# A rarely taken branch moved from the middle of a mixture-of-experts kernel to its end, and four gathers moved within GpSimd's order

## The chip, the cores and the metric

The kernel runs on one core of a Trainium2 chip. The core has TensorE (PE: matmuls, and PEld: weight loads), VectorE (DVE), ScalarE (ACT), GpSimd (POOL) and SyncE (SP, which issues the transfers), each with its own instruction stream. The metric is the device time of one execution in microseconds (us); lower is better.

## The reference

Pooled attention over 4 batches of 576 tokens gives `x` of 2304 rows and 512 columns. A mixture of 8 experts follows, of which each token takes its best two, then a dense mixture of 4 experts. All is float32.

```python
# attention: k and v averaged over 8 neighbours, softmax(q k / 8) v -> x [2304, 512]
logits = x @ w_gate
noisy_logits = logits + np.log1p(np.exp(x @ w_noise)) * noise
top2 = np.argpartition(-noisy_logits, 2, axis=1)[:, :2]   # softmax of the two -> top2_w
for e in range(8):                                        # first mixture
    for k in range(2):
        mask = top2[:, k] == e
        h = np.maximum(x[mask] @ w1[e], 0.0)              # 512 -> 1024
        out[mask] += top2_w[mask, k, None] * (h @ w2[e])  # 1024 -> 512
for e in range(4):                                        # second mixture, x is out
    out2 += p[:, e:e + 1] * (np.maximum(x @ w1[e], 0.0) @ w2[e])
```

## The kernel before, in words

**Stages.** Attention writes `x` to a buffer `x_d` in memory. A routing step on VectorE finds each token's two experts and gives it a slot in a table of 8 times 640 slots (`CAP`). Then come chunks, one after the other: tokens of one expert are gathered from `x_d` by GpSimd (`fetch1`, which calls `gather`), turned by TensorE (`turn_full`, `turn_plain`), multiplied by the expert's first matrix (layer 1), passed through the maximum with 0, and multiplied by the second (layer 2). Results of the first mixture go to a buffer `y_d`; `fetch2` gathers two rows for each token from it and `mix2` adds them. The second mixture works on three groups of 768 tokens and stores `out` (line 1144).

**Operands in two parts.** Each float32 operand is split into a rounded part and a remainder, and three products of them are summed. For weights, ScalarE writes the rounded part and GpSimd (or VectorE) subtracts it for the remainder. Some chunks use seven products of half matrices in place of eight (`run_seven`, `layer1_seven`): for these GpSimd first combines quarters of the weights in a tile `comb` (lines 561 to 564), ScalarE rounds (lines 566 and 574), and GpSimd subtracts (lines 570 to 580). First-layer weights lie in a ring of three tiles, `u0`, `u1` and `u2` (`u_161`, `u_162` and `u_163` in the rows of the program's order); second-layer weights lie in `v` and `v_last`.

**What sets the order.** The program is written out by hand: each engine executes its instructions in the order in which the Python code emits them. A chunk has two halves, each a row of places `u`; `add(h, u, f, ...)` enters a call at half `h`, place `u`. `ahead_plain` and the tables `AHEAD_1`, `AHEAD_2` say at which place which part of the next weights is split. `step` takes a routing generator to its next `yield`, so a `yield` more shifts what comes behind it by one place. SyncE waits, in order, for the data of each transfer that it issues.

**The branch.** If an expert gets more tokens than slots, the table doesn't hold them. The routing writes a flag `over` (line 473), and `general` (line 1111) reads it on each engine and, if it is set, runs `all_experts`, a loop over all tokens and all experts. `between` holds it until the matmuls of the second product of expert 7's first chunk are emitted (lines 697 and 1117). On the path on which the flag is 0, TensorE, VectorE and SyncE add to their semaphores what the skipped block would have added; SyncE does this with eight increments, one for each semaphore of its transfers. In the profiled execution the flag is 0.

**The gathers of expert 3.** Line 1088 enters four of its five gathers at place (0, 4) of the second chunk of expert 1, so they stand ahead of the weight splits of the next chunk, expert 2. Their turns are at places 8 to 14 of expert 2's first half.

Of the kernel before, what the change touches and what calls it, by code (L numbers as in the profile page):

```python
# [8 lines left out]
FT = mybir.dt.float32  # L9
# [6 lines left out]
OP = mybir.AluOpType  # L16
# [7 lines left out]
N, DM = B * S, H * D  # L24
F = 1024
E1, E2 = 8, 4
# [5 lines left out]
CAP = SLOT_TILES * 128  # L32
# [27 lines left out]
def tile_attention_moe_moe(  # L60
# [12 lines left out]
    nc = tc.nc  # L73
# [6 lines left out]

    dram = ctx.enter_context(tc.tile_pool(name="dram", bufs=1, space=DRAM))
    x_d = dram.tile([N, DM], FT, name="x_d")
    wd_d = dram.tile([N, E1], FT, name="wd_d")
    y_d = dram.tile([E1 * CAP, DM], FT, name="y_d")
    psr = ctx.enter_context(tc.tile_pool(name="psr", bufs=2, space=PSUM, side="right"))

    consts = pool(ctx, "consts", 1)
# [244 lines left out]
    over = consts.tile([128, 1], I32, name="over")  # L332
# [8 lines left out]
    def routing(g, hold):  # L341
# [120 lines left out]
        if g == EARLY - 1 or last:  # L462
            slots[last] = consts.tile([128, HC], I32, name=f"slots{int(last)}")
            nc.vector.tensor_scalar(slots[last], slotf, float((N if last else GROUPS[EARLY] * 128) - 1), None, op0=OP.min)
            for e in range(1 if last else SPLIT):
                for c in range(3 if last else 2):
                    fetch1(e, 2 + c if last else c, not last)
            yield
        nc.vector.scalar_tensor_tensor(rows[:, a:b], ei[:, a:b], float(CAP), pf, op0=OP.mult, op1=OP.add)
        yield  # L470
        if last:
# [209 lines left out]
    def bank():  # L681
        return pm.tile([128, 512], FT, name="wn", bufs=4)

    between = []

    def layer1(q, f, xa, xb, n, bank=bank, hs=None):

        w = pair_weights(q, f // 2)
        p = bank()[:, :n]
        i = 0  # L690
        for a, b in TERMS:
            for kd in range(KD):
                qu = (0 if f % 2 else 1) if kd < 2 else (3 if f % 2 else 2)
                nc.tensor.matmul(p, w[:, a, qu, (kd % 2) * 128:(kd % 2 + 1) * 128],  # L694
                                 xc[(xa, xb)[kd // 2]][:, b, kd % 2, :n], start=i == 0, stop=i == 11)
                i += 1
        while between:
            between.pop()()
        relu_split(f, 0, n, p, hs)()

    h_first, y_first = [], []
# [252 lines left out]
    def run_seven(n, sink, fills):  # L954
        subs = 2 * n // 128
        for h in range(2):
            q = at_half[0]
            fl = {k[1]: list(f) for k, f in fills.items() if k[0] == h}
            for u, plan in (AHEAD_2 if n == CA else AHEAD_1).items():
                for i, k in plan:  # L960
                    fl.setdefault(u, []).append(lambda i=i, k=k: w_step(4 * q + i, k, None, False))
            w_step(4 * q + 2, 9)
            for pr in range(2):
                layer1_seven(q, pr, n, fl, 7 * pr)
                w_at["used1"] += 1
            for t in range(subs):
                for f in fl.get(14 + t, ()):
                    f()
                step(3, 1)
                sink(h, t, layer2(q, t))  # L970
            w_at["used2"] += 2
            at_half[0] += 1


    def new_acc():
        return moe.tile([128, DM], FT, name="acc", bufs=6)
# [27 lines left out]
    def all_experts():  # L1004

        wd, oh = (sx[i][:, 0, 0:NT * E1].rearrange("p (t e) -> p t e", e=E1) for i in range(2))
        for k in range(2):
            o = oh if k else wd
            nc.vector.tensor_tensor(o, exp_i.unsqueeze(1).to_broadcast([128, NT, E1]),
                                    ei[:, :, k].unsqueeze(2).to_broadcast([128, NT, E1]), op=OP.is_equal)  # L1010
            nc.vector.tensor_tensor(o, o, wt2[:, :, k].unsqueeze(2).to_broadcast([128, NT, E1]), op=OP.mult)
        nc.vector.tensor_add(wd, wd, oh)
        nc.sync.dma_start(wd_d.rearrange("(t p) e -> p t e", p=128), wd)
        x, xT, w0, w1, h0, h1 = (xf[0].rearrange("p k c -> p (k c)")[:, i * 512:(i + 1) * 512] for i in range(6))
        y = new_acc()
        wt = consts.tile([128, E1], FT, name="wd_t")
        with tc.For_i(0, N, 128) as r:
            nc.sync.dma_start(x, x_d[bass.ds(r, 128), :])
            nc.sync.dma_start(wt, wd_d[bass.ds(r, 128), :])
            p = psr.tile([128, 512], FT, name="tr")  # L1020
            for kd in range(KD):
                nc.tensor.transpose(p[:, kd * 128:(kd + 1) * 128], x[:, kd * 128:(kd + 1) * 128], ident)
            nc.vector.tensor_copy(xT, p)
            nc.vector.memset(y, 0.0)
            for e in range(E1):
                for f in range(FB):
                    w = (w0, w1)[f % 2]
                    if f % 2:
                        nc.sync.dma_start(w[:, 0:256], wa[e, 0][:, f - 1, 0:256])
                        nc.sync.dma_start(w[:, 256:512], wa[e, 0][:, f, 256:512])  # L1030
                    else:
                        nc.sync.dma_start(w[:, 0:256], wa[e, 0][:, f, 256:512])
                        nc.sync.dma_start(w[:, 256:512], wa[e, 0][:, f + 1, 0:256])
                    p = psr.tile([128, 512], FT, name="tr")
                    for kd in range(KD):
                        nc.tensor.matmul(p[:, :128], w[:, kd * 128:(kd + 1) * 128],
                                         xT[:, kd * 128:(kd + 1) * 128], start=kd == 0, stop=kd == KD - 1)
                    nc.vector.tensor_scalar((h0, h1)[f // 4][:, (f % 4) * 128:(f % 4 + 1) * 128], p[:, :128],
                                            0.0, None, op0=OP.max)
                p = pm.tile([128, 512], FT, name="p2", bufs=2)  # L1040
                for f in range(FB):
                    w = (w0, w1)[f % 2]
                    nc.sync.dma_start(w, wa[e, 1][:, f])
                    nc.tensor.matmul(p, (h0, h1)[f // 4][:, (f % 4) * 128:(f % 4 + 1) * 128], w,
                                     start=f == 0, stop=f == FB - 1)
                nc.vector.scalar_tensor_tensor(y, p, wt[:, e:e + 1], y, op0=OP.mult, op1=OP.add)
            nc.sync.dma_start(y_d[bass.ds(r, 128), :], y)
        nc.vector.memset(wt2[:, :, 0], 1.0)
        nc.vector.memset(wt2[:, :, 1], 0.0)
        for k in range(2):  # L1050
            nc.vector.tensor_scalar(rows[:, :, k], tok_i, float(N // 2), None, op0=OP.add)

    fills = {}

    def add(h, u, f, *a):
        fills.setdefault((h, u), []).append(lambda: f(*a))
# [28 lines left out]
    add(0, 1, turn_full, (2, 3), 3)  # L1085
    add(0, 2, turn_full, (2, 4), 4)
    for c in range(4):
        add(0, 4, fetch1, 3, c)
    for k, at_k in enumerate(((0, 3), (0, 4), (0, 4), (0, 5))):
        add(*at_k, sums, CS, (k,))  # L1090
    for m, at_m in zip(ORDER, ((0, 6), (1, 4), (1, 0), (1, 5), (1, 1), (1, 2), (1, 3))):
# [2 lines left out]
    for e in range(2, E1 - 1):  # L1094
# [13 lines left out]
                add(0, 0, fetch1, e + 1, c)  # L1108
                add(1, 14 + c, turn_plain, (e + 1, c), (S1, S2), c)
        run_seven(CS, sink1(e, 0), fills)  # L1110
    def general():
        with tc.If(nc.values_load(over[0:1, 0:1], min_val=0, max_val=1) != 0):  # L1112
            all_experts()

    e = E1 - 1
    fills.clear()
    add(0, 1, between.append, general)
    for c in range(2):
        add(0, 0, fetch1, e, 3 + c)
        add(0, 4 + c, turn_plain, (e, 3 + c), (S3, S4), c)  # L1120
# [12 lines left out]
    def sink2(e, accs, c0, first, last):  # L1133
        def sink(h, t, p):
            tok = c0 + t
            w = pe[:, tok, e:e + 1]
            if first and h == 0:
                accs[tok] = new_acc()
                nc.vector.tensor_scalar(accs[tok], p, w, None, op0=OP.mult)
            else:  # L1140
                a = accs[tok]
                nc.vector.scalar_tensor_tensor(a, p, w, a, op0=OP.mult, op1=OP.add)  # L1142
                if last and h:
                    nc.sync.dma_start(out[tok * 128:(tok + 1) * 128, :], a)
        return sink
# [19 lines left out]
    for sc in range(3):  # L1165
        es = range(1 if sc == 0 else 0, E2)
        for e in es:
            fills.clear()
            k = e - es[0]
            if sc < 2 and k < 2:  # L1170
                a, b, c = (6 * (sc + 1) + 3 * k + i for i in range(3))
                for t, f, m, u in ((a, (0, 10), (0, 16), (0, 17)), (b, (0, 10), (0, 17), (0, 18)),
                                   (c, (0, 19), (1, 14), (1, 15))):
                    add(*f, fetch2, t)
                    add(*m, mix2, t)
                    add(*u, turn2, t)
            if sc < 2 and e == E2 - 1:
                add(0, 18, sums, CA)
                window(CA)
            run_seven(CA, sink2(e, accs, 6 * sc, e == 0, e == E2 - 1), fills)  # L1180


def arrays_of(i):
# [44 lines left out]
```

## Time and profile before

| | |
|---|---|
| three runs | 1309.9, 1314.5, 1314.6 us, median 1314.5 |
| the profiled execution | 1311.17 us, its span 1309.4 us |
| TensorE matmul, weight load busy | 98%, 88% of the span |
| VectorE, ScalarE, GpSimd busy | 54%, 44%, 65% |
| transfers | 156.18 MB, 119 GB/s in the mean |
| granted TensorE clock | 0.998 of the full one |

The span reaches from the first to the last instruction of the program; the execution's own time has 1.8 us more around it. A busy share says little about the end of the time, as the stages have other limits each; below, stretches are looked at one by one. A "q" behind an engine's name (PEldq, SPq) is its sequencer, which issues instructions and is not counted as busy.

### The profile page before, as it was taken

Reading aid. Unit: us, or ns where it says so; the run is one execution under the profiler, and the core shown is the slowest. Engines: PE = TensorE matmul, PEld = TensorE weight load, DVE = VectorE, ACT = ScalarE, POOL = GpSimd, SP = SyncE. Lnnn points to the kernel's source line nnn. Section 1 sums busy time; section 2 is a strip of 40 time slices with the busy share of each in tenths; the row PEclk is TensorE's granted clock in tenths of the full one; section 3 lists DMA queues with packets and bytes.
Section 4 is the critical chain, followed back from the end, with each engine's and each line's share of the span. In section 5 each row is a group of like instructions: output and inputs, shape, how many; then the busy total and the mean of one; then the engine's idle time right before and its main releaser. Section 6 shows DMA issues by size and latency. Waiting matters only on the chain.

```text
span 1309.4 us, 19496 instructions
## 1 busy us (share of the span) xinstructions
PE 1288.7 (98%) x7408; PEld 1153.9 (88%) x7408; DVE 711.5 (54%) x1269; ACT 570.6 (44%) x1046; POOL 848.1 (65%) x777
## 2 busy tenths in 40 slices
PE   8989999999999999999999999999999999999998
PEld 6778998898998898999999998999899889999997
DVE  6766336557475542666545457545444664444444
ACT  5865545645456334644434334433333433333331
POOL 5757679788797846316867556767566576555560
PEclk9999999999999999999999999999999999999999
DMA  9765564243442444744423223323222232222201
GB/s 359 250 163 163 184 203 145 88 161 104 127 157 80 145 136 122 244 160 131 127 65 114 67 78 113 113 65 113 65 65 67 71 121 65 76 70 65 65 17 48
DMA packets 59556, 156.18 MB, mean 119 GB/s; under 512 B 18240, under 2 KB 20032, under 8 KB 58304
## 3 DMA queue, kind: packets, MB, share of 16 engines
q1 hardware_dynamic: 53376, 134.94, 32.3%
q0 software_dynamic: 6080, 19.93, 4.9%
q8 instruction: 60, 0.98, 0.3%
q14 instruction: 40, 0.33, 0.1%
HBM read 134.92 MB, written 19.92 MB: 118 GB/s over the span
## 4 chain that ended last, share of the span: by engine, by line
PE 59%; DVE 2%; ACT 1%; issue 0%; ACTq 0%
PE p L905 30%; PE wn L859 23%; PE wn L694 4%; DVE x L658 1%; PE tr L616 1%; DVE acc L1142 0%; ACT hs L672 0%; ACT x L655 0%; DVE hs L673 0%; DVE wn L889 0%; DVE wn L880 0%; ACT u L574 0%; DVE gat L999 0%; ACT u L566 0%; ACT gat L998 0%
## 5 line engine op out<-in xcount | busy, mean ns | idle before, releaser
L859 PE MATMUL wn<-x,u 128*128 128x384 f32 (+1 forms) x2688 | 453.1, 327 | 1.7 <-DVE u L877 1.0
L859 PEld LDWEIGHTS wn<-x,u 128*128 128x128 f32 x2688 | 445.6, 188 | 5.1 <-DVE u L877 1.3
L905 PE MATMUL p<-v,hs 128*128 128x512 f32 x1740 | 428.3, 392 | 1.2 <-DVE hs L673 0.6
L905 PEld LDWEIGHTS p<-v,hs 128*128 128x128 f32 x1740 | 323.2, 188 | 70.1 <-DVE hs L673 2.9
L672 ACT ACTIVATE hs<-wn 128x384 fp32r<-128x384 f32 (+2 forms) x312 | 144.2, 471 | 276.7 <-DVE wn L880 146.3
L905 PE MATMUL p<-v_last,hs 128*128 128x512 f32 x900 | 230.8, 391 | 1.1 <-DVE hs L673 0.6
L673 DVE SCALAR_TENSOR_TENSOR hs<-wn,hs 128x384 fp32r<-128x384 f32 (+2 forms) x312 | 160.4, 530 | 120.8 <-ACT hs L672 114.4
L905 PEld LDWEIGHTS p<-v_last,hs 128*128 128x128 f32 x900 | 167.8, 188 | 36.6 <-DVE hs L673 1.5
L1142 DVE SCALAR_TENSOR_TENSOR acc<-p,pe,acc 128x512 f32<-128x512 f32 x126 | 94.5, 750 | 189.9 <-PE p L905 189.8
L557 POOL TENSOR_TENSOR v<-w_st,v 128x1024 fp32r<-128x1024 f32 x41 | 101.9, 2485 | 120.4 <-ACT v L551 120.3
L580 POOL TENSOR_TENSOR u<-comb,u 128x1024 fp32r<-128x1024 f32 x60 | 149.7, 2494 | 45.3 <-ACT u L574 45.0
L572 POOL TENSOR_TENSOR u<-w_st,u 128x768 fp32r<-128x768 f32 x60 | 114.0, 1901 | 49.2 <-ACT u L566 49.2
L551 ACT ACTIVATE v<-w_st 128x1024 fp32r<-128x1024 f32 x64 | 67.5, 1057 | 170.7 <-PE p L905 161.8
L694 PE MATMUL wn<-x,u 128*128 128x384 f32 (+1 forms) x672 | 110.8, 321 | 1.5 <-PEq L1112 1.5
L694 PEld LDWEIGHTS wn<-x,u 128*128 128x128 f32 x672 | 107.2, 189 | 2.9 <-issue 1.8
L557 POOL TENSOR_TENSOR v_last<-w_st,v_last 128x1024 fp32r<-128x1024 f32 x22 | 55.2, 2508 | 47.9 <-ACT v_last L551 47.9
L574 ACT ACTIVATE u<-comb 128x1024 fp32r<-128x1024 f32 x64 | 67.5, 1054 | 27.6 <-POOL comb L564 27.6
L555 POOL TENSOR_TENSOR u<-w_st,u 128x256 fp32r<-128x256 f32 x80 | 57.5, 750 | 33.3 <-ACT u L551 19.9
L874 DVE TENSOR_TENSOR u<-wn,u 128x384 f32<-128x384 f32 (+1 forms) x64 | 34.3, 537 | 75.1 <-PE wn L859 40.4
L561 POOL TENSOR_TENSOR comb<-w_st 128x256 f32<-128x256 f32 x64 | 47.9, 748 | 33.1 <-DMA w_st<-wb 31.0
L551 ACT ACTIVATE v_last<-w_st 128x1024 fp32r<-128x1024 f32 x32 | 33.8, 1056 | 75.6 <-PE p L905 75.6
L604 POOL DMA_INDIRECT gat<-y_d,rows x36 | 36.5, 1014 | 36.4 <-DVE hs L673 12.7
(153 smaller groups left out, 1330.4 us busy)
## 6 DMA issues: line engine op xcount, KB each, us to landing
w_st<-wb SPq DMA_DIRECT2D x104, 512.0 KB, 3.9
w_st<-wa SPq DMA_DIRECT2D x88, 512.0 KB, 4.1
y_d<-acc SPq DMA_DIRECT2D x38, 256.0 KB, 3.7
x_d<-xs SPq DMA_DIRECT2D x18, 256.0 KB, 4.9
out<-acc SPq DMA_DIRECT2D x18, 256.0 KB, 2.1
k_st<-kt SPq DMA_DIRECT2D x3, 1152.0 KB, 13.7
v_st<-vt SPq DMA_DIRECT2D x3, 1152.0 KB, 11.7
q_sb<-qt SPq DMA_DIRECT2D x3, 1152.0 KB, 12.7
```

Of the source, the lines that this page charges most:

```text
L551: nc.scalar.activation(w[:, 0], st, AF.Copy)
L555: eng.tensor_sub(w[:, 1, i], st[:, i], w[:, 0, i].bitcast(FT))
L557: eng.tensor_sub(w[:, 1], st, w[:, 0].bitcast(FT))
L572: nc.gpsimd.tensor_sub(w[:, 1, 0:3], st[:, 1:4], w[:, 0, 0:3].bitcast(FT))
L574: nc.scalar.activation(w[:, 0, 3:7], t, AF.Copy)
L580: nc.gpsimd.tensor_sub(w[:, 1, 3:7], t, w[:, 0, 3:7].bitcast(FT))
L672: nc.scalar.activation(hi, p, AF.Relu)
L673: return lambda: nc.vector.scalar_tensor_tensor(hs[:, 1, f, c0:c0 + n], p, 0.0, hi.bitcast(FT), op0=OP.max, op1=OP.subtract)
L694: nc.tensor.matmul(p, w[:, a, qu, (kd % 2) * 128:(kd % 2 + 1) * 128], xc[(xa, xb)[kd // 2]][:, b, kd % 2, :n], start=i == 0, stop=i == 11)
L859: nc.tensor.matmul(p, w[:, a, wm, kd * 128:(kd + 1) * 128], xc[xm][:, b, kd, :n], start=first and i == 0, stop=i == 5, skip_group_check=True)
L905: nc.tensor.matmul(p, hs[:, a, f, t * 128:(t + 1) * 128], w[:, b, f % 2], start=f == 0 and i == 0, stop=f == FB // 2 - 1 and i == 2)
L1142: nc.vector.scalar_tensor_tensor(a, p, w, a, op0=OP.mult, op1=OP.add)
```

## The change

The call of `all_experts` moves behind the last product of the second mixture, so the branch is the last thing in the program. As nothing follows it, the block now computes both mixtures and stores `out` itself; the routing clamps the slot number to 639 (`CAP - 1`), so that rows beyond the table are not addressed on the way there. The four gathers of expert 3 move from place (0, 4) to (1, 6), the last place of the chunk.

```diff
+        nc.vector.tensor_scalar(pf, pf, float(CAP - 1), None, op0=OP.min)
+        yield
         nc.vector.scalar_tensor_tensor(rows[:, a:b], ei[:, a:b], float(CAP), pf, op0=OP.mult, op1=OP.add)
...
-        while between:
-            between.pop()()
         relu_split(f, 0, n, p, hs)()
...
+        def mixture(src, o, v, n, c0):
...
+        with tc.For_i(0, N, 128) as r:
+            nc.sync.dma_start(x, x_d[bass.ds(r, 128), :])
+            nc.sync.dma_start(wt, wd_d[bass.ds(r, 128), :])
+            mixture(x, y, wa, E1, 0)
+            mixture(y, z, wb, E2, E1)
+            nc.sync.dma_start(out[bass.ds(r, 128), :], z)
...
     for c in range(4):
-        add(0, 4, fetch1, 3, c)
+        add(1, 6, fetch1, 3, c)
...
-    add(0, 1, between.append, general)
...
             run_seven(CA, sink2(e, accs, 6 * sc, e == 0, e == E2 - 1), fills)
+    with tc.If(nc.values_load(over[0:1, 0:1], min_val=0, max_val=1) != 0):
+        all_experts()
```

In TensorE's order before, the branch stands between the products of expert 7's first chunk (`wn` is a product's sum; the rows from line 1017 on are the block that is skipped).

```order
L694 MATMUL wn<-x_1364,u_161 128x384 x2
L694 MATMUL wn<-x_1363,u_161 128x384 x2
L694 MATMUL wn<-x_1364,u_161 128x384 x2
L1112 TENSOR_LOAD over
L1112 COMPARE_AND_BRANCH
L1017 COMPARE_AND_BRANCH
L1017 UNCONDITIONAL_BRANCH x2
```

Here the products now follow each other without a break. SyncE's order at the end of the changed program (`w_st` receives weights, `acc` holds the sums of the second mixture; the rows from line 1012 on are skipped):

```order
L1138 DMA out<-acc 128x512 x2
L537 DMA w_st<-wb 128x1024 x25
L1138 DMA out<-acc 128x512 x6
L1175 TENSOR_LOAD over
L1175 ISA x2
L1175 COMPARE_AND_BRANCH
L1012 DMA wd_d<-sx_1996 128x18x8
L1013 DMA wd_d<-pe 128x18x4
```

The load, two register operations and the branch, which stood among the weight loads of expert 7, now stand behind the six last stores. GpSimd's order before, in the second chunk of expert 1, with the gathers (`gat`) ahead of the splits for expert 2:

```order
L555 TENSOR_TENSOR u_163<-w_st,u_163 128x256 x4
L604 DMA gat<-x_d,slots_2058 128x512 x4
L555 TENSOR_TENSOR u_161<-w_st,u_161 128x256 x4
L561 TENSOR_TENSOR comb<-w_st 128x256
L562 TENSOR_TENSOR comb<-w_st,comb 128x256
L563 TENSOR_TENSOR comb<-w_st 128x256
L564 TENSOR_TENSOR comb<-w_st,comb 128x256
L570 TENSOR_TENSOR u_162<-w_st,u_162 128x256 x3
L578 TENSOR_TENSOR u_162<-comb,u_162 128x256 x4
```

And GpSimd's order in the changed program, whose line numbers here are two higher, from the split of `u_162` on:

```order
L572 TENSOR_TENSOR u_162<-w_st,u_162 128x256 x3
L580 TENSOR_TENSOR u_162<-comb,u_162 128x256 x4
L563 TENSOR_TENSOR comb<-w_st 128x256
L564 TENSOR_TENSOR comb<-w_st,comb 128x256
L565 TENSOR_TENSOR comb<-w_st 128x256
L566 TENSOR_TENSOR comb<-w_st,comb 128x256
L572 TENSOR_TENSOR u_163<-w_st,u_163 128x256 x3
L580 TENSOR_TENSOR u_163<-comb,u_163 128x256 x4
L606 DMA gat<-x_d,slots_2059 128x512 x4
L559 TENSOR_TENSOR v_last<-w_st,v_last 128x1024
L563 TENSOR_TENSOR comb<-w_st 128x256
```

The four gathers have moved past two sets of combinations and the splits of `u_161`, `u_162` and `u_163`; `v_last` and the third set follow them. On VectorE the remainder of the hidden layer (`hs`, now line 675, before line 673) has moved ahead of three small operations of the routing's end:

```order
L838 RECIPROCAL wt_2000<-cw_d 128x18
L675 SCALAR_TENSOR_TENSOR hs<-wn,hs 128x256
L840 TENSOR_TENSOR wt_2000<-wt_2000 128x18
L841 TENSOR_REDUCE cw_d<-probs 128x18
L842 TENSOR_SCALAR cw_d<-cw_d 128x18
L844 RECIPROCAL cw_d<-cw_d 128x18
L845 TENSOR_TENSOR pe<-probs,cw_d 128x72
```

Before, it stood between the operation of line 844 on `cw_d` and the reciprocal of line 846 behind it.

## Rows read from the trace of the kernel before

**Rows 1.** Engines by stretch (from:to, length, then busy us and count each).

```profile
240.00:486.00 246.00, 246.00 (x1385) 222.07 (x1385) 151.42 (x236) 122.66 (x215) 192.49 (x137) 1.00 0.38 122
```

**Rows 2.** TensorE in order of time (start, length; idle time before), after the branch.

```profile
493.41 4.40 PE L694 MATMUL wn<-x,u 128*128 128x384 f32 x24 [1.54 <-PEq L1112]
```

**Rows 3.** TensorE in order of time, first products of expert 2.

```profile
220.26 2.90 PE L859 MATMUL wn<-x,u 128*128 128x320 f32 x18 [1.03 <-DVE u L877]
223.00 0.60 PE L616 MATMUL tr<-ident,gat 128*128 128x128 f32 x4
...
227.32 1.15 PE L859 MATMUL wn<-x,u 128*128 128x320 f32 x6 [0.47 <-ACT u L871]
```

**Rows 4.** TensorE in order of time, layer 2 while the routing ends.

```profile
126.77 1.28 PE L905 MATMUL p<-v_last,hs 128*128 128x512 f32 x4 [0.58 <-DVE hs L673]
```

**Rows 5.** SyncE's last stores in order of time, and its waits behind them by line.

```profile
1292.86 13.93 SPq L1144 DMA_DIRECT2D out<-acc  x6
...
L1224 SPq EVENT_SEMAPHORE  x11: 17/28/28, 1306.8 to 1307.4; - x11
...
L1224 SPq EVENT_SEMAPHORE  x1: 28/28/28, 1308.4 to 1308.4; - x1
```

**Rows 6.** Line 1112: count, duration ns min/median/max, first and last start us.

```profile
L1112 PEldq COMPARE_BRANCH  x1: 4043/4043/4043, 489.2 to 489.2; - x1
...
L1112 SPq TENSOR_LOAD <-over x1: 488/488/488, 490.8 to 490.8; - x1
L1112 DVEq COMPARE_BRANCH  x1: 72/72/72, 491.0 to 491.0; - x1
...
L1112 DVEq EVENT_SEMAPHORE  x1: 21/21/21, 491.6 to 491.6; - x1
L1112 SPq COMPARE_BRANCH  x1: 50/50/50, 491.7 to 491.7; - x1
```

**Rows 7.** Line 1112, SyncE's increments, in two short windows.

```profile
L1112 SPq EVENT_SEMAPHORE  x6: 17/17/17, 495.0 to 495.5; - x6
...
L1112 SPq EVENT_SEMAPHORE  x2: 17/17/17, 496.9 to 497.0; - x2
```

**Rows 8.** SyncE in order of time, transfers around the branch.

```profile
490.39 7.16 SPq L535 DMA_DIRECT2D w_st<-wa  x2
```

**Rows 9.** The page's transfers: count, size, median us to landing.

```profile
w_st<-wa SPq DMA_DIRECT2D x88, 512.0 KB, 4.1
```

**Rows 10.** GpSimd in order of time, around the four gathers.

```profile
187.43 2.01 POOL L555 TENSOR_TENSOR u<-w_st,u 128x256 fp32r<-128x256 f32 x2
...
194.18 0.94 POOL L604 DMA_INDIRECT gat<-x_d,slots  x1 [0.30 <-PE p L905]
195.13 3.50 POOL L555 TENSOR_TENSOR u<-w_st,u 128x256 fp32r<-128x256 f32 x4
...
201.56 1.32 POOL L563 TENSOR_TENSOR comb<-w_st 128x256 f32<-128x256 f32 x1
202.85 1.72 POOL L564 TENSOR_TENSOR comb<-w_st,comb 128x256 f32<-128x256 f32 x1
204.53 2.72 POOL L570 TENSOR_TENSOR u<-w_st,u 128x256 fp32r<-128x256 f32 x3
...
225.12 0.73 POOL L564 TENSOR_TENSOR comb<-w_st,comb 128x256 f32<-128x256 f32 x1
```

**Rows 11.** ScalarE in order of time, its part of the splits.

```profile
199.84 0.84 ACT L566 ACTIVATE u<-w_st 128x768 fp32r<-128x768 f32 x1
...
214.77 1.06 ACT L574 ACTIVATE u<-comb 128x1024 fp32r<-128x1024 f32 x1 [5.73 <-POOL comb L564]
...
225.88 1.06 ACT L574 ACTIVATE u<-comb 128x1024 fp32r<-128x1024 f32 x1 [1.68 <-POOL comb L564]
```

**Rows 12.** Line 604, the four gathers: issue to landing.

```profile
DMA to landing us min/median/max: 3.5/3.7/4.3
```

**Rows 13.** Line 469, the operation behind the clamp.

```profile
L469 DVE SCALAR_TENSOR_TENSOR rows<-ei,g_pf x2: 215/493/771, 82.3 to 122.8; 128x18 int32<-128x18 f32 x2
```

More of the change, by code (lines that the diff above doesn't have):

```diff
@@ L82, in tile_attention_moe_moe @@
     x_d = dram.tile([N, DM], FT, name="x_d")
-    wd_d = dram.tile([N, E1], FT, name="wd_d")
+    wd_d = dram.tile([N, E1 + E2], FT, name="wd_d")
     y_d = dram.tile([E1 * CAP, DM], FT, name="y_d")
@@ L682, in bank @@
         return pm.tile([128, 512], FT, name="wn", bufs=4)
-    between = []
     def layer1(q, f, xa, xb, n, bank=bank, hs=None):
@@ L1012, in all_experts @@
         nc.vector.tensor_add(wd, wd, oh)
-        nc.sync.dma_start(wd_d.rearrange("(t p) e -> p t e", p=128), wd)
+        to = wd_d.rearrange("(t p) e -> p t e", p=128)
+        nc.sync.dma_start(to[:, :, 0:E1], wd)
+        nc.sync.dma_start(to[:, :, E1:E1 + E2], pe)
         x, xT, w0, w1, h0, h1 = (xf[0].rearrange("p k c -> p (k c)")[:, i * 512:(i + 1) * 512] for i in range(6))
[L1015 to L1019, printed above, removed]
+        y, z = new_acc(), new_acc()
+        wt = consts.tile([128, E1 + E2], FT, name="wd_t")
+        def mixture(src, o, v, n, c0):
             p = psr.tile([128, 512], FT, name="tr")
             for kd in range(KD):
-                nc.tensor.transpose(p[:, kd * 128:(kd + 1) * 128], x[:, kd * 128:(kd + 1) * 128], ident)
+                nc.tensor.transpose(p[:, kd * 128:(kd + 1) * 128], src[:, kd * 128:(kd + 1) * 128], ident)
             nc.vector.tensor_copy(xT, p)
-            nc.vector.memset(y, 0.0)
-            for e in range(E1):
+            nc.vector.memset(o, 0.0)
+            for e in range(n):
                 for f in range(FB):
                     w = (w0, w1)[f % 2]
[L1028 to L1033, printed above, removed]
+                    a, b = (f - 1, f) if f % 2 else (f, f + 1)
+                    c = 0 if f % 2 else 256
+                    nc.sync.dma_start(w[:, 0:256], v[e, 0][:, a, c:c + 256])
+                    nc.sync.dma_start(w[:, 256:512], v[e, 0][:, b, 256 - c:512 - c])
                     p = psr.tile([128, 512], FT, name="tr")
@@ L1042, in all_experts @@
                     w = (w0, w1)[f % 2]
-                    nc.sync.dma_start(w, wa[e, 1][:, f])
+                    nc.sync.dma_start(w, v[e, 1][:, f])
                     nc.tensor.matmul(p, (h0, h1)[f // 4][:, (f % 4) * 128:(f % 4 + 1) * 128], w,
                                      start=f == 0, stop=f == FB - 1)
[L1046 to L1051, printed above, removed]
+                nc.vector.scalar_tensor_tensor(o, p, wt[:, c0 + e:c0 + e + 1], o, op0=OP.mult, op1=OP.add)
+        with tc.For_i(0, N, 128) as r:
[4 more added lines that the diff above has]
+            nc.sync.dma_start(out[bass.ds(r, 128), :], z)
     fills = {}
@@ L1110, in tile_attention_moe_moe @@
         run_seven(CS, sink1(e, 0), fills)
-    def general():
-        with tc.If(nc.values_load(over[0:1, 0:1], min_val=0, max_val=1) != 0):
-            all_experts()
     e = E1 - 1
     fills.clear()
-    add(0, 1, between.append, general)
     for c in range(2):
```

## The prediction

> **What bounds the kernel now.** I first read how busy each engine is by stretch, since a page's share over the whole span mixes stages with different limits. From 240 to 486 us TensorE's matmuls fill 246.00 of 246 us [rows 1]: whatever makes them late before that stays lost until the end, and whatever frees them is won. So I went through the places where TensorE stood still near the lines that change, in the instructions in order of time, and there are three. At the branch it stands 1.54 us, released by its own sequencer [rows 2]. In expert 2's first products it stands 1.03 us for VectorE and 0.47 us for ScalarE [rows 3]. At 126.77 it stands 0.58 us for VectorE [rows 4]. Last I read the end: SyncE issues the last store until 1292.86 + 13.93 = 1306.79, its next eleven waits stand 0.06 us apart, the last is met at 1308.4 when that store has landed, and the span ends at 1309.4, 1.0 us later [rows 5]. Nothing runs on another engine there: this end is SyncE's alone, and what is added behind the last store is added to the time.
>
> **Taking the branch out of the middle.** The reader is to see in the rows of line 1112 that each engine loads the flag, branches, and goes on behind the skipped block [rows 6]. TensorE's branch takes 4.04 us, from 489.2 to 493.2. Its sequencer runs ahead of its matmuls, so 2.5 us of that lies beside the product already queued, and 1.54 us is seen [rows 2, 6]. The product behind it used weights that were ready. Taken out: -1.5 us. Bounds: 0, if the product then waits for something else, and -1.54. VectorE, ScalarE and GpSimd lose nothing here that TensorE waited for.
>
> **Putting it behind the last product.** SyncE now does, after its last store, what it did in the middle. From the start of its load (490.8) to the first of eight semaphore increments (495.0) it took 4.2 us; six increments stand within 0.5 us, and the last two come only at 496.9 to 497.0, after a pause of some 1.4 us [rows 6, 7]. Eight at the pitch of the six are 0.7 us, so the block costs 4.9 us without the pause and 6.2 us with it. Afterwards stand twelve waits at 0.06 us (0.7 us, all met by then) and the same 1.0 us to the end. From 1306.8: 1306.8 + 4.9 + 0.7 + 1.0 = 1313.4 against 1309.4, that is +4.0 us; with the pause +5.3. The landing of the store (1308.4) now lies beside the branch and is no cover for the rest. TensorE's branch is over 1.5 us behind its matmuls, as in the middle, and these end before the last store is issued, so it is over by 1308.3; VectorE goes on 0.6 us after its branch begins (491.0 to 491.6) [rows 6]. Both are earlier than SyncE.
>
> Why 3.3 us pass between SyncE's branch (491.7) and its first increment [rows 6] can be read in two ways. It may be the jump itself. Or the first increment, which also waits for SyncE's earlier transfers, waited for the one issued at 490.39, whose like take 4.1 us to land [rows 8, 9]. On the second reading only 0.6 us as on VectorE is the jump, and at the end the landing hides most: 1306.8 + 0.9 + 0.6 = 1308.3, increments to 1309.0, then 1.7, so 1310.7 or +1.3. TensorE's row decides me for the first: its 4.04 us contain no transfer. The low bound of this step stays +1.3, the high one +5.3; I take +4.0.
>
> [...]
>
> **The four gathers of expert 3.** GpSimd issues them between 189.44 and 195.13, 5.7 us, ahead of all the weight splits of expert 2 [rows 10]. In the new order they stand behind the splits of u_162 and u_163, directly ahead of v_last. So the splits may start earlier, but not all by 5.7 us: those of u_162 (line 570) need ScalarE's line 566, which ends at 199.84 + 0.84 = 200.68 and is held by TensorE's products, not by GpSimd [rows 11]. GpSimd reaches it early (190 + 3.5 for four splits + at most 6.0 for four combinations = 199.5) and idles. Line 570 starts at 200.7 instead of 204.53: 3.85 us won, 1.85 us of idle time lost.
>
> From 204.53 to the end of the third set of combinations at 225.12 + 0.73 = 225.85 GpSimd works without a gap for 21.3 us. In the new order the same work plus the gathers ends at 200.7 + 21.3 + gathers. Undisturbed, a gather takes 0.94 us and 0.30 us ahead of it, so four take 5.0 us: 227.0, or +1.2 us. As slow as now (5.7 us) they make it +1.9. The splits of u_162 also move into a time when VectorE runs its own large splits: the combinations that now stand there took 1.32 and 1.72 us against 0.73 for the same size when undisturbed [rows 10], 1.6 us too much, and line 570 would take that over: +2.8 us, and +3.5 with slow gathers.
>
> [...]
>
> What waits for it: ScalarE's line 574 is held for that third set (it starts at 225.88, released by GpSimd), its line 871 stands behind it, and TensorE's product at 227.32 is released by line 871 [rows 3, 11]. So this product starts at about 230.1. The wait of 1.03 us at 220.26 hangs in the same way on the second set (line 574 at 214.77) and disappears, since that set comes earlier, but TensorE only arrives earlier at the next wait, which becomes some 4.3 us instead of 0.47. Net +2.8 us. The gathers land 3.5 to 4.3 us after issue, the first issued near 218.5, so at 222 to 223; its transpose stands at 223.00 now and comes some 1.0 us earlier then [rows 3, 12]: a wait below 1 us, swallowed by the longer one behind it. Bounds: -1.5 (both waits vanish and GpSimd is not late) and +3.5.
>
> **The clamp.** Two more VectorE operations of 128x18; the one behind each took 0.2 and 0.8 us [rows 13], so 0.2 to 0.8 each. The first, at 82 us, holds nobody. The second pushes what TensorE waits for at 126.77, but the extra step also moves the hidden layer's remainder (line 673) ahead of three small operations, of about 1 us together. I take 0, between -0.5 and +0.5. General path's own code does not run.
>
> **Sum.** -1.5 + 4.0 + 2.8 + 0 = +5.3 us. The profiled execution took 1311.17 us, 1.8 us around a span of 1309.4; so 1316.5 on its basis. The three runs before lie at 1309.9, 1314.5 and 1314.6, the median 3.3 us above the profiled one, with no cause in the program. On the median the sum is 1319.8. I predict between the two, 1318.5 us.
>
> **Rivals.** (1) The gathers cost nothing: if GpSimd is fast enough (line 566 comes earlier, no slow neighbours), both waits go: -1.5 + 4.0 - 1.5 = +1.0 us, or 1314. For it: the second set really comes earlier. Against: GpSimd has no gap from 189 to 226, and idle time is put in. (2) The end is hidden by the landing: -1.5 + 1.3 + 2.8 = +2.6 us, or 1315.8. For it: the coincidence of 490.39 plus 4 us with 495.0. Against: TensorE's 4.04 us. With (1) it would be -1.7 us, the best case. (3) Slower beyond what can be told: SyncE's end takes the pause of its increments too, a second stop in the same block. Place: between the increments or right behind them; price 1.4 us, so -1.5 + 5.3 + 2.8 = +6.6 us, and +7.3 with slow gathers: 1321 to 1322 on the median. It decides once SyncE needs over 6 us from its load to its last increment. For it: the middle did just that. [...]
>
> **Chances and range.** Within 0.5% (6.6 us) of 1314.5 I cannot tell a change of this kernel from none. Forecast 0.50, rival 1 0.15, rival 2 0.13, rival 3 0.22. The forecast's own range is 1315 to 1322. The range for 8 in 10 takes in the bounds of gathers and end and the scatter of the runs (4.7 us): 1311.5 to 1324. Slower: nearly all of rival 3 and a quarter of the forecast, 0.33. Faster needs the best case and a favourable run: 0.03. The same: 0.64.
>
> **What would show it.** No stop of TensorE at expert 7's second product. GpSimd idle of 1 to 3 us before line 572 (570 before), the gathers at 218 to 224. One stop of TensorE of about 4 us before a product near 230, and the ones near 218 to 220 gone. At the end, from SyncE's last issue to the end of the span, 6.6 us instead of 2.6. Wrong would be: no gap on GpSimd, a stop near 230 below 1 us, or an end that lasts no longer than now; and a general path that is entered.

## The result and the profile after

The changed kernel takes 1330.7 us (median of 4 runs, 1328.9 to 1333.4), the kernel before 1313.8 us beside it (4 runs, 1309.9 to 1314.6): a ratio of 1.0137, 95% interval 1.0107 to 1.0166, or 18 us slower by the ratio (the two medians lie 16.9 apart). The forecast was 1318.5 us in a range of 1311.5 to 1324; the time lies above the range. The profiled execution has a span of 1327.1 us against 1309.4, at nearly the same granted clock (0.996 and 0.998 of the full one as means over the span), 17.7 us more.

I read the trace of after at the places of the prediction first, then between them.

**The branch has left the middle.** TensorE in order of time, at the place of [rows 2]:

```profile
493.04 1.56 PE L903 MATMUL p<-v_last,hs 128*128 128x512 f32 x6
494.44 8.51 PE L694 MATMUL wn<-x,u 128*128 128x384 f32 x48
```

All 48 products of expert 7's first layer stand in one row without a stop; the 1.54 us are gone. If the n-th matmul of after is set beside the n-th of before, which shows how far TensorE lags, the lag falls by 1.8 us at this place. A stop is counted from the end of the product before it, and products overlap (six second-layer products last 1.52 us in before, and the next six start 1.36 us after these did), so the starts lose some 0.2 us more than the stop shows.

**The end.** SyncE's last stores in order of time, then instructions by line (1175 is the branch, 1220 the program's end; engine first, then count, duration in ns, first and last start), in answer to [rows 5 to 7]:

```profile
1306.88 14.33 SPq L1138 DMA_DIRECT2D out<-acc  x6
```

```profile
L1175 SPq EVENT_SEMAPHORE  x8: 17/17/17, 1324.9 to 1325.4; - x8
...
L1175 ACTq COMPARE_BRANCH  x1: 50/50/50, 1304.4 to 1304.4; - x1
...
L1175 PEldq COMPARE_BRANCH  x1: 3367/3367/3367, 1316.5 to 1316.5; - x1
...
L1175 SPq TENSOR_LOAD <-over x1: 521/521/521, 1321.3 to 1321.3; - x1
...
L1175 SPq COMPARE_BRANCH  x1: 50/50/50, 1322.2 to 1322.2; - x1
...
L1220 SPq EVENT_SEMAPHORE  x14: 17/28/28, 1325.5 to 1327.1; - x14
```

The last store is issued until 1306.88 + 14.33 = 1321.2, and the span ends at 1327.1: 5.9 us instead of 2.6, +3.3. The load starts at once, the branch at 1322.2, and 2.7 us pass until the first increment at 1324.9. All eight stand within 0.5 us; the pause that [rows 7] show is not there. TensorE's branch (3.4 us from 1316.5) is over before.

**The gathers.** GpSimd and then TensorE in order of time, in answer to [rows 10] and [rows 3]:

```profile
202.49 3.94 POOL L572 TENSOR_TENSOR u<-w_st,u 128x256 fp32r<-128x256 f32 x3 [3.27 <-ACT u L568]
...
219.92 0.96 POOL L606 DMA_INDIRECT gat<-x_d,slots  x1
221.19 0.95 POOL L606 DMA_INDIRECT gat<-x_d,slots  x1 [0.30 <-issue]
...
229.18 0.73 POOL L566 TENSOR_TENSOR comb<-w_st,comb 128x256 f32<-128x256 f32 x1
```

```profile
224.38 0.85 PE L618 MATMUL tr<-ident,gat 128*128 128x128 f32 x4 [2.04 <-DMA gat<-x_d,slots]
224.89 3.44 PE L857 MATMUL wn<-x,u 128*128 128x320 f32 x12
...
231.38 1.15 PE L857 MATMUL wn<-x,u 128*128 128x320 f32 x6 [1.74 <-ACT u L869]
```

And a stop of before, a little ahead of [rows 3], that after does not have:

```profile
208.46 0.50 PE L905 MATMUL p<-v,hs 128*128 128x512 f32 x1 [0.62 <-DVE hs L673]
```

GpSimd waits 3.27 us for ScalarE (1 to 3 were foreseen), the gathers stand at 220, and the wait of 1.03 us is gone. TensorE now stops twice, 2.04 us for the first gather's landing (issued at 219.92, used at 224.38) and 1.74 us behind the combinations, and between the two it is slow: 12 products take 3.44 us, where 18 took 2.90 before [rows 3]. By the n-th matmul TensorE is 1.7 us behind at 205 us of before, 0.8 us ahead at 220 and 4.1 us behind at 229. So it gains 2.5 us (the stops of 1.03 and 0.62 us and a small one between them, each with its overlap) and loses 4.9 us: +2.3 for the gathers.

**And everywhere else.** These three make -1.8 + 3.3 + 2.3 = +3.8 us. Another +0.9 us is there from the first 25 us on, where nothing was changed. 13.0 of the 17.7 us are missing. They are in no stop. Engines by stretch (from:to, length, busy us and count of TensorE's matmuls, its weight loads, VectorE, ScalarE, GpSimd; granted clock, DMA share, GB/s), before and then after, the first row of after answering to [rows 1]:

```profile
620.00:1280.00 660.00, 658.93 (x3335) 595.25 (x3334) 334.75 (x539) 236.59 (x376) 426.22 (x319) 1.00 0.26 80
```

```profile
240.00:486.00 246.00, 246.00 (x1377) 219.76 (x1375) 149.17 (x232) 122.62 (x214) 190.72 (x136) 1.00 0.38 121
620.00:1280.00 660.00, 659.50 (x3299) 589.62 (x3298) 334.09 (x537) 236.79 (x375) 430.84 (x323) 1.00 0.27 81
```

TensorE is as busy as before (659.50 of 660 us against 658.93), at a granted clock of 1.00 in both rows, and gets less done: 3299 matmuls in 660 us instead of 3335. At 0.198 us each the 36 missing ones are 7.1 us in this stretch alone. Which ones are dearer is seen in the last products (TensorE in order of time; each row is six matmuls), before and then after:

```profile
1302.76 1.52 PE L905 MATMUL p<-v,hs 128*128 128x512 f32 x6
1304.12 1.52 PE L905 MATMUL p<-v_last,hs 128*128 128x512 f32 x6
```

```profile
1317.10 1.56 PE L903 MATMUL p<-v,hs 128*128 128x512 f32 x6
1318.50 1.56 PE L903 MATMUL p<-v_last,hs 128*128 128x512 f32 x6
```

Six matmuls of the second layer take 1.36 us from start to start before (226.7 ns each) and 1.40 us after (233.3 ns). Over all of them behind 620 us the mean distance of two starts grows from 229.6 to 234.7 ns (worked out from some 1550 starts in each trace), 5.1 ns; with 2640 such matmuls in the kernel that is 13.5 us. The first layer's products (128x384) stay at 173.6 to 173.8 ns in the same stretch.

What had changed for the second layer? Neither its instructions nor their order. But the diff widens one constant tile, wd_t, from 8 to 12 columns, which the general path alone uses. In the built program its place grows from 32 to 64 bytes per partition (the tiles around it lie at multiples of 32), and every tile that lies behind it on the same side of the memory moves by 32 bytes: hs, the second layer's stationary operand, from byte 63488 to 63520, and with it the accumulators, the temporaries and some of the first layer's operands. The weight tiles v and v_last, which stream past it, lie on the other side and stay.

### The profile page after: what moved, and what is told of

The parts are those of the page before. It is cut to its first block, busy times and chain, and to the rows that moved or that the text cites. A ratio compares the mean times of both kernels' runs of the same rounds, so it can differ in the third digit from the quotient of the medians.

```text
span 1327.1 us, 19491 instructions
## 1 busy us (share of the span) xinstructions
PE 1304.2 (98%) x7408; PEld 1156.4 (87%) x7408; DVE 711.2 (54%) x1271; ACT 571.3 (43%) x1046; POOL 849.0 (64%) x777
## 4 chain that ended last, share of the span: by engine, by line
PE 90%; DVE 5%; POOL 2%; ACT 1%; issue 1%; DMA 0%; SPq 0%; DVEq 0%; ACTq 0%; POOLq 0%
PE p L903 44%; PE wn L857 32%; PE wn L694 7%; PE tr L618 2%; PE pv L289 2%; DVE x L660 1%; PE s L252 1%; PE et L279 1%; PE s L694 1%; POOL u L580 0%; DMA k_st<-kt 0%; DVE acc L1136 0%; POOL u L572 0%; DVE oh_lo L441 0%; ACT hs L674 0%
## 5 line engine op out<-in xcount | busy, mean ns | idle before, releaser
L903 PE MATMUL p<-v,hs 128*128 128x512 f32 x1740 | 436.8, 397 | 0.2 <-DVE acc L1136 0.2
L903 PE MATMUL p<-v_last,hs 128*128 128x512 f32 x900 | 235.8, 397 | 0.7 <-DVE hs L675 0.4
```

The source lines that it names most:

```text
L903: nc.tensor.matmul(p, hs[:, a, f, t * 128:(t + 1) * 128], w[:, b, f % 2], start=f == 0 and i == 0, stop=f == FB // 2 - 1 and i == 2)
```

## Experiments

Two theories at first. **Addresses:** the 32 bytes make the second layer dearer, by some 13 us. **Code:** the longer general path, the gathers or the moved branch do it, wherever the tiles lie. Times are medians; a ratio is to the kernel before, run beside.

**1. The change with the old addresses (after_aligned).**

```diff
-    consts.tile([128, LEFT], FT, name="left")
+    left = consts.tile([128, LEFT], FT, name="left")
...
-        wt = consts.tile([128, E1 + E2], FT, name="wd_t")
+        consts.tile([128, E1], FT, name="wd_t")
+        wt = left[:, 0:E1 + E2]
```

> The kernel after, with the 12-column tile of the general path's weights laid into a constant tile that is there but unused, and an 8-column tile left in its old place: every SBUF address is that of the kernel before, all other code is that of after. Addresses (theory A: the 32 bytes by which the wider tile moves every tile of the left side behind it, the stationary operand hs of the second layer among them, make each 128x512 product dearer): the pitch of these products goes back from 233 to 227 ns, the profiled span falls by about 13 to 14 us to 1313-1314, and the time is 4 to 5 us above the kernel before. Code (theory B: the longer, moved general path or the gathers slow the products, wherever the tiles lie): pitch 233 ns and 16 to 18 us above before, as after.

Measured: 1318.5 us, ratio 1.0045 (1.0032 to 1.0057), +5.9 us. TensorE's last products:

```profile
1305.66 1.52 PE L903 MATMUL p<-v,hs 128*128 128x512 f32 x6
1307.02 1.52 PE L903 MATMUL p<-v_last,hs 128*128 128x512 f32 x6
```

1.36 us for six again. With the whole change in place and only the tiles put back, 12 of the 18 us are gone. The theory of code falls for these 12; the 5.9 that are left are the subject of experiment 6.

**2. The kernel before with the new addresses (before_wide_tile).**

```diff
-        wt = consts.tile([128, E1], FT, name="wd_t")
+        wt = consts.tile([128, E1 + E2], FT, name="wd_t")[:, 0:E1]
```

> The kernel before with the tile of the general path's weights 12 columns wide in place of 8, of which 8 are used: nothing else differs, and no instruction is added. Addresses: pitch 233 ns in the second layer and 13 to 14 us above before (about 1327). Code: 227 ns and no change (within 3 us of before).

Measured: 1326.2 us, ratio 1.0101 (1.0080 to 1.0123), +13.3 us, and 1.40 us for six:

```profile
1317.97 1.56 PE L905 MATMUL p<-v,hs 128*128 128x512 f32 x6
1319.37 1.56 PE L905 MATMUL p<-v_last,hs 128*128 128x512 f32 x6
```

Four columns that nobody uses cost what was missing.

**3. Which tile (before_pad_hs, before_wide_pad_hs).**

```diff
+    moe.tile([128, 8], FT, name="pad")
     hs = moe.tile([128, 2, FB // 2, CW], FR, name="hs")
```

> The kernel before with an unused tile of 32 bytes right ahead of hs: hs, the accumulators and the temporaries of the first layer's seven products move by 32 bytes, the activations' tiles x0, x2, x4, xf and the sums stay. If it is hs as the stationary operand of the second layer: 13 to 14 us above before, pitch 233 ns. If it is the activations (or their readers on VectorE, ScalarE and GpSimd): no change, 227 ns. By the theory of code: no change.

Measured: 1324.8 us, ratio 1.0096 (1.0074 to 1.0118), +12.6 us, 1.40 us for six:

```profile
1315.37 1.56 PE L906 MATMUL p<-v,hs 128*128 128x512 f32 x6
1316.77 1.56 PE L906 MATMUL p<-v_last,hs 128*128 128x512 f32 x6
```

The activations' tiles stayed, so it is hs (or, moved with it, the accumulators and temporaries, which TensorE doesn't read).

> The kernel before with the 12-column tile and the unused 32 bytes ahead of hs: everything from the tile on moves by 32 bytes, but hs, the accumulators and the temporaries by 64. If hs has to lie at a multiple of 64 bytes: pitch 227 ns and no change (within 3 us of before), though all other tiles lie as in after. If any move away from the old place costs, or if the activations' tiles are it: 233 ns and 10 us or more above before.

Measured: 1324.6 us, ratio 1.0093 (1.0071 to 1.0116), +12.2 us, again 1.40 us for six:

```profile
1316.26 1.56 PE L906 MATMUL p<-v,hs 128*128 128x512 f32 x6
1317.66 1.56 PE L906 MATMUL p<-v_last,hs 128*128 128x512 f32 x6
```

I had thought of lines of 64 bytes; that falls. At +64 hs is as slow as at +32.

**4. How wide the pattern is (pad_128, pad_256, pad_512),** the same edit with 32, 64 and 128 columns, one execution each, so what is read is the distance of two starts and not the time.

> The kernel before with an unused tile of 128 bytes ahead of hs (32 and 64 bytes gave 233 ns per product against 227). If the weight load reads hs in lines of 128 bytes and pays for a slice that straddles one: 227 ns, span as before (1309). If it is a wider alignment, or the old address itself: 233 ns and 13 us more.

> The kernel before with an unused tile of 256 bytes ahead of hs, between 128 (233 ns, slow) and 512 (227 ns, as before). If the pattern repeats every 256 bytes: 227 ns and 1311 us; if only every 512: about 232 ns and 1322 us.

> The kernel before with an unused tile of 512 bytes ahead of hs. Every slice of hs that is loaded is 512 bytes wide and begins at a multiple of 512 bytes from the start of hs. If what counts is the alignment of a slice (to anything up to 512 bytes): 227 ns and 1309 us. If it is the place of hs against the moving operand in some larger pattern, or the old address itself: 233 ns and 1322 us.

TensorE's last products with 128, 256 and 512 bytes:

```profile
1314.33 1.56 PE L906 MATMUL p<-v,hs 128*128 128x512 f32 x6
1315.72 1.56 PE L906 MATMUL p<-v_last,hs 128*128 128x512 f32 x6
```

```profile
1308.21 1.52 PE L906 MATMUL p<-v,hs 128*128 128x512 f32 x6
1309.57 1.52 PE L906 MATMUL p<-v_last,hs 128*128 128x512 f32 x6
```

```profile
1305.84 1.52 PE L906 MATMUL p<-v,hs 128*128 128x512 f32 x6
1307.20 1.52 PE L906 MATMUL p<-v_last,hs 128*128 128x512 f32 x6
```

At +128 bytes it is slow (1.39 us; span 1321.1), at +256 and +512 fast (1.36 us; spans 1314.8 and 1312.5). So the old address as such is nothing special. The values fit a pattern that repeats every 256 bytes; places beyond 128 that are no multiple of 256 were not tried. (pad_256's span is 5 us above before at the same pitch of the products; where 4 of these 5 us are is told in the last section.)

**5. hs by itself, or hs against the moving operand (edge_32, edge_32_pad_32).** An unused tile at the other end of the memory is made 32 bytes smaller, which moves the weight tiles; then hs as well.

```diff
-    edge.tile([128, EDGE], FT, name="edge")
+    edge.tile([128, EDGE - 8], FT, name="edge")
...
+    moe.tile([128, 8], FT, name="pad")     # in edge_32_pad_32 alone
     hs = moe.tile([128, 2, FB // 2, CW], FR, name="hs")
```

> The kernel before with the unused tile at the other end of the memory 32 bytes smaller: the moving operand of the second layer (the weight tiles v) and the stationary one of the first move by 32 bytes, hs stays. If only the alignment of hs itself counts: second layer 227 ns, and the first layer's products (173 ns, their stationary operand moved) dearer by some nanoseconds if the alignment of any stationary operand counts. If it is the place of hs against the moving operand: 233 ns in the second layer.

> As edge_32, and with 32 unused bytes ahead of hs, so that hs and the weight tiles move alike. If it is the place of hs against the moving operand: 227 ns again. If it is the alignment of hs itself: 233 ns.

edge_32, then edge_32_pad_32:

```profile
1318.97 1.56 PE L905 MATMUL p<-v,hs 128*128 128x512 f32 x6
1320.37 1.56 PE L905 MATMUL p<-v_last,hs 128*128 128x512 f32 x6
```

```profile
1305.48 1.52 PE L906 MATMUL p<-v,hs 128*128 128x512 f32 x6
1306.84 1.52 PE L906 MATMUL p<-v_last,hs 128*128 128x512 f32 x6
```

With hs at its old place and the weights moved it is slow (span 1325.7); with both moved by 32 bytes it is fast (1312.1). The accumulators and temporaries stay in the first and move with hs in the second, so they are not it. What counts is the distance of the two operands, not the place of either: moved alike, or by 256 or 512 bytes against each other, they keep 227 ns; 32, 64 or 128 bytes against each other make it 232 to 233 ns. Why, no run here shows.

**6. The rest of the change, at the old addresses.** The gathers back in their old place; then also the branch left out; then, with the branch, the last stores from another engine.

```diff
-        add(1, 6, fetch1, 3, c)
+        add(0, 4, fetch1, 3, c)
```

> after_aligned with the four gathers of expert 3 back in their old place (the first half's fourth slot); the branch stays at the end. If the late gathers cost what the trace of after shows (TensorE's lag on before grows by 2.3 us between 200 and 229 us): 2.3 us less than after_aligned, 1316 us, and no idle of 2 us before the first turn of expert 3. If they cost nothing: 1318.5. The rest above before is then the branch: 3.3 at the end less 1.5 in the middle, 1.8 us.

Measured: 1318.4 us beside 1316.2 for before (before took 3.6 us more on this chip than beside after_aligned), ratio 1.0016 (1.0003 to 1.0028), +2.1 us: 3.8 us below after_aligned by the ratios, whose intervals leave 1.5 to 6. The trace is sharper. If the n-th matmul of a kernel is set beside the n-th of before, TensorE's lag from 200 to 229 us grows by 2.30 us in after_aligned and by 0.01 us here, and 1.8 us come back in both, as in after, where the branch was. First expert 2's transpose of after_aligned, then the same products here:

```profile
225.07 1.08 PE L618 MATMUL tr<-ident,gat 128*128 128x128 f32 x4 [2.52 <-DMA gat<-x_d,slots]
...
231.60 1.15 PE L857 MATMUL wn<-x,u 128*128 128x320 f32 x6 [1.31 <-ACT u L869]
```

```profile
226.18 2.90 PE L857 MATMUL wn<-x,u 128*128 128x320 f32 x18 [1.03 <-DVE u L875]
...
233.23 1.15 PE L857 MATMUL wn<-x,u 128*128 128x320 f32 x6 [0.48 <-ACT u L869]
```

The stops of [rows 3] are back, within 0.01 us.

```diff
-    with tc.If(nc.values_load(over[0:1, 0:1], min_val=0, max_val=1) != 0):
-        all_experts()
+    consts.tile([128, E1], FT, name="wd_t")
```

> aligned_early_gathers without the branch and without the general path (left out altogether; it isn't taken with these inputs), tiles where before has them. If the branch at the end costs the 3.3 us by which the stretch from the last store's issue to the end grew: 1312.7 us, that is 3.3 below aligned_early_gathers and 1.5 below before, since before pays for the branch in the middle. If the end is set by the landing of the last store: no change against aligned_early_gathers.

Measured: 1315.0 us, ratio 0.9992 (0.9981 to 1.0003), 3.4 us below aligned_early_gathers and 1.1 below before, the latter not to be told from none. SyncE's last stores:

```profile
1297.94 13.93 SPq L1139 DMA_DIRECT2D out<-acc  x6
```

They are issued until 1311.87, the span ends at 1314.4: 2.5 us. In aligned_early_gathers:

```profile
1297.03 13.93 SPq L1139 DMA_DIRECT2D out<-acc  x6
```

So until 1310.96, and the span ends at 1316.7: 5.7 us. The branch at the end costs 3.2 us. From SyncE's load (1311.0) to its last increment (1315.0) it takes 4.0 us, and the twelve waits behind it 0.7 us; 1.6 us of this lie beside the landing of the last store, which the end waits for without a branch too.

```diff
-                    nc.sync.dma_start(out[tok * 128:(tok + 1) * 128, :], a)
+                    (nc.scalar if c0 == 12 else nc.sync).dma_start(out[tok * 128:(tok + 1) * 128, :], a)
```

> aligned_early_gathers with the last six stores of the output issued by ScalarE in place of SyncE (and the general path's store with them). SyncE then reaches the branch early and its jump (2.7 us) lies beside the last products; ScalarE's own jump took 0.13 us in after. If SyncE's jump behind its last store is the price of the branch: 3 us less than aligned_early_gathers, 1313, and the end 2.6 to 3 us after the last store's issue. If every engine's jump counts or the landing sets the end: the same as aligned_early_gathers.

Measured: 1316.7 us, ratio 1.0004 (0.9994 to 1.0014), 1.7 us below aligned_early_gathers, not the 3 expected. The last stores and the branch by line:

```profile
L1139 ACTq DMA_DIRECT2D out<-acc x6: 338/338/386, 1294.3 to 1307.9; - x6
...
DMA to landing us min/median/max: 2.8/4.6/5.2
```

```profile
L1176 SPq EVENT_SEMAPHORE  x8: 17/17/17, 1251.8 to 1310.7; - x8
...
L1176 SPq COMPARE_BRANCH  x1: 50/50/50, 1248.7 to 1248.7; - x1
```

SyncE branches at 1248.7, 60 us early, and its 3.1 us to the first of the eight are off the path. But the eight turn out to be waits too: the last stands at 1310.7, when the last store (issued until 1308.2) has landed, and the twelve waits of the end come behind it. The end is 4.2 us instead of 2.6, so the branch still costs 1.6 us: no shorter landing than 2.8 us is seen here, against 2.0 in before, and the twelve waits (0.06 us each, 0.7 us) had been met beforehand there. Why the last store lands later where a branch stands at the end (2.9 us in after and aligned_early_gathers, 2.8 here; 2.0 in before and without the branch) was not tried.

No version beats the kernel before by what can be measured; without any branch the gain is 1.1 us, not to be told from none. Of the versions with the branch at the end, aligned_stores_on_scalar is the fastest, level with before; it has the gathers in their old place. The late gathers only cost time, 2.3 us by the trace.

## Why the prediction was wrong, by its own steps

- **Branch out of the middle, -1.5:** right. The stop of [rows 2] is gone; by the n-th matmul TensorE gets back 1.8 us in after and in the aligned kernels alike, a little over the bound of 1.54, by the overlap of products told above.
- **Branch behind the last store, +4.0:** right in its mechanism, +3.3 in after, +3.2 by leaving the branch out. The 0.7 us are in SyncE's jump, 2.7 us instead of the 3.3 from [rows 6]; the jump and not a landing sets it, as TensorE's row had decided: in after the last store has landed at 1323.8, 2.9 us after its issue, and the first increment stands at 1324.9. With the branch at the end the jump takes 2.5 to 3.1 us on SyncE (2.5 in aligned_early_gathers, 2.7 in after, 3.1 in aligned_stores_on_scalar), 3.4 us on TensorE in after and 3.8 us in the other two, and 0.1 us on ScalarE in after (line 1220 starts at 1304.6 after the branch at 1304.4). What sets its length, no run shows.
- **Gathers, +2.8:** +2.3. GpSimd's idle time (3.27 us; 1 to 3 were foreseen), the longer splits of line 572 (3.94 us in place of 2.72, so +1.2 where +1.6 had been estimated from [rows 10]) and the vanished stop of 1.03 us came as worked out. The gathers were on time too: after is 1.7 us behind before by then, so 219.92 there is about the 218.5 of the working. What it lacked is that TensorE comes earlier, since the stop of 0.62 us at 208.46, which the working left out, goes too. So the one stop of 4.3 us was split, and TensorE waited 2.04 us for the first gather where I had written below 1 us. That the sum still comes to nearly +2.8 is in part luck.
- **Clamp, 0:** right. The stop of [rows 4] is 0.41 us in after instead of 0.58, and TensorE comes out of the stretch 0.2 us later, within the bounds.
- **Rivals:** 1 (gathers for nothing) and 2 (end hidden by the landing) are refuted by the stops above and by aligned_no_branch. Rival 3's second stop of SyncE did not come. None of the three holds what happened.
- **The step that failed is one that the sum did not have.** Of the new 12-column tile I counted what uses it, and nothing uses it in this run. I did not count what it moves. That term is +13.3 us (10.5 to 16.1, before_wide_tile), three times the largest that I had, and it alone takes the time out of the range. The whole sum rests on the durations of before holding for after, product by product; for 2640 of them they did not. The addresses stand in the built program of after, so this could have been seen ahead; its price could not, since no row of before shows the second layer at another distance.

With the tiles put back, the change takes 1318.5 us where 1318.5 was forecast. That the two are equal is in part luck: the forecast was laid between two bases, 1311.2 and 1314.5, and before measured 1312.6 beside after_aligned. The sum of the terms that it had was +5.3; after_aligned measures +5.9 (4.2 to 7.5), of which the trace shows 3.1 (its end takes 5.7 us) + 2.3 - 1.8 = 3.6 at the places of the change. Its span is 6.0 us longer than that of before. Of the other 2.4 us, 2.0 are there at 130 us already, where of the whole change only the clamp has run; their cause stays open.

## What to carry to other kernels

Here a tile 16 bytes larger moved every tile behind it by 32, and that cost 13.3 us (before_wide_tile): compare the allocations of both built programs before taking old durations for new, above all the distance between the stationary and the moving operand of the products that fill TensorE. Where TensorE is busy to 100% in both traces and the span differs, count instructions per stretch and the distance of two starts: 13.0 of the 17.7 us here were in no stop. The branch at the end cost 3.2 us where SyncE issued the last stores, and 1.6 us where ScalarE did; ask which engine has something to do last, read the jump from that engine's own branch row and put it behind work that ends earlier.

## What the runs showed of the hardware

- **Distance of operands.** The 128x512 fp32r products of the second layer took 226.7 ns from start to start where the stationary operand begins a multiple of 256 bytes from where the moving one begins (by the built programs; their strides are multiples of 256 here; measured in before, in edge_32_pad_32 with both moved alike, and in pad_256 and pad_512) and 232 to 233 ns where it is off by 32 bytes (after, before_wide_tile, before_pad_hs, edge_32), by 64 (before_wide_pad_hs) or by 128 (pad_128): 2.9% of each product, 1% of this kernel. The products of the first layer, 128x384, moved hardly at all (173.6 ns in before, 174.6 ns in edge_32, with their stationary operand 32 bytes off some of the moving ones).
- **A part of the spread between executions** has a place. Engines by stretch (columns as above), in before and then in pad_256, whose products have the same pitch:

```profile
86.00:92.00 6.00, 6.00 (x90) 5.13 (x91) 3.45 (x11) 4.32 (x15) 5.46 (x12) 1.00 0.54 163
92.00:98.00 6.00, 6.00 (x60) 5.77 (x60) 3.34 (x11) 1.94 (x4) 2.14 (x8) 1.00 0.89 216
```

```profile
86.00:92.00 6.00, 4.04 (x52) 2.86 (x51) 2.50 (x8) 2.63 (x12) 5.44 (x10) 1.00 0.69 206
92.00:98.00 6.00, 6.00 (x69) 5.54 (x68) 2.78 (x9) 2.36 (x7) 1.52 (x6) 0.72 0.72 178
```

  In pad_256 TensorE stands 2 us between 86 and 92, and the clock granted in the next 6 us is 0.72 of the full one; it has lost 4.0 us there against before. All four kernels profiled on that chip (pad_256 and the three with the gathers back) lost between 1.5 and 4.1 us at this place, whatever their edit; the nine other profiles lost nothing there. On that chip the kernel before itself goes with the clock: its eight executions at 0.999 or more of the full clock have spans of 1310.8 to 1312.8 us, its ten at 0.996 or less 1315.0 to 1317.9. So a single profile of this kernel can't tell 4 us from none by its span, and the ratios and the stops above are read instead.
